# An attention kernel with a convolutional MoE layer behind it: the MoE begins at attention step 31, not 26, with its first-layer units 0.8 steps apart

## The chip, the core and the metric

One core of one Trainium2 chip runs the whole program. The time is device microseconds of one execution, from launch to end; the median of three runs is compared. A profile of one further execution is read beside it. Its five engines each work through a queue in order: PE (matmul; PEld is its weight load), DVE (vector), ACT (activations, copies out of PSUM), POOL (elementwise work in SBUF) and SP (issues DMAs).

## What is computed

Attention with rotary positions over 4 batches, 8 heads, 576 tokens, head width 64; its output, regrouped to 4 x 576 x 512, goes through a feed-forward layer with a gate that comes from a convolution over three neighbouring tokens:

```python
    q_rot, k_rot = (rotate(q), rotate(k))
    scores = scale * np.matmul(q_rot, k_rot.transpose(0, 1, 3, 2))
    scores = scores - np.max(scores, axis=-1, keepdims=True)
    attn = np.exp(scores)
    attn = attn / (np.sum(attn, axis=-1, keepdims=True) + 1e-09)
    return np.matmul(attn, v).astype(np.float32)
...
    h = np.maximum(x @ w_in, 0.0)
...
    for k in range(K):
        conv_out += conv_w[k][None, None, :] * hp[:, k:k + S, :]
    gate = 1.0 / (1.0 + np.exp(-conv_out))
    return (h * gate @ w_out).astype(np.float32)
```

All inputs are float32 but the three weight tensors of the layer, which arrive as 64-bit floats and are converted on the chip.

## The kernel before

**Attention steps.** The heads are taken two at a time: 16 pairs, numbered p, four to a batch. A pair takes five steps, s = 0 to 4, so that attention is steps n = 5p + s, 0 to 79. Step n holds the scores of 128 query rows (64 rows of both heads for s = 4) against all 576 keys (`emit_S`, L206 and L229, tile sp), a negated maximum on DVE (`reds`, L214, tile negm), the exponential with its sum on ACT (`exps`, L218, tile st), and the transposes of the exponentials of the step before (`emit_T`, L263, tile tp; ACT copies them out into pt at L162). In five steps there are also the transposes of the next pair's q, remainder and k (`emit_TQ`, L185 and L175), remainders (`emit_Trem`, L275 and L280, copied out by DVE), two products with v (`emit_E`, L316, for p in steps 5p+4 and 5p+5), the reciprocal of the sums and its way through HBM (`emit_rinv`, `emit_rinvT`, tiles sums, rvc, rst, rb), and in step 5p+8 the normalisation of both halves of the result (`norms`, L328, tile xn on DVE), which ACT and POOL split into the two parts of xT (L332, L333). POOL turns the next pair's q, r and k (`rope`, L143 to L156) eight and six steps ahead. Steps whose PE work has a product with v are called E steps below; they are two of every five.

**Slots of x.** xT has 12 slots of 128 columns of x by one half (290 tokens) of a batch. A normalisation takes a slot from `free_slots`, and the last first-layer unit of a block gives its four back (L349 to L351).

**The MoE.** A block is half of a batch, 288 tokens; there are eight. A block has eight first-layer units, M1 (`emit_M1`, f = 0 to 7): twelve matmuls with 290 columns (L347), Relu on ACT into one of four rr tiles (L355), and then, a number of ticks later by `lag`, the convolution on DVE (L359 once, L361 twice), tanh on ACT (L367), the gate on DVE (L370), and the split into g on ACT and POOL (L378, L379). Its second layer comes in units M2 (`emit_M2`) of six matmuls with 512 columns (L425), four units to a tile of 128 tokens; the tile stays in one of the two PSUM buffers of the pool m from its first unit to its fourth, when DVE copies it out (L432, tile ot).

**The order.** The whole program is written out in the order of a table: `at(n, rank, fn)` puts work into step n, and within a step the ranks sort it. Every engine works its queue in that order, with no later rearrangement. Until step WIDE the scores use a PSUM layout with 512 columns to a matmul and are emitted one step ahead; PSUM then has no pool m. During those steps the weights are converted in 16 pieces (`conv_w_piece`): an Abs on ACT (L443), four operations on DVE (L446, L452, L455, L460), and a copy on ACT and a subtraction on POOL (L503, L504). These units are spread evenly over steps 0 to WIDE-2 (`wsteps`). From WIDE on the scores take 288 columns to a matmul, the PSUM pool m is there, and MoE block number blk (of the first six) has its M1 units at n0+1+f and the M2 units of the block before from n0, with n0 = WIDE + 10 blk. Units of one step are spread between its transposes and products. The last two blocks come behind all of this (`seq`, `second`), all first-layer units and then all second-layer units.

**The convolution's weights.** `conv_cw` converts them (one Abs on ACT, four small operations on DVE, 32 x 128), and `turn_cw` turns them on PE (L524) and copies them out on DVE (L525).

The lines that the change touches are in this table's code:

```python
            for i, u in enumerate(wsteps):
                x = (WIDE - 1) * i // nw
                at(x, 0.4, u)
            at(12, 3, conv_cw)
            at(14, 2, turn_cw)
...
                us = [(n0 + 1 + f, lambda blk=blk, f=f: emit_M1(blk, f)) for f in range(NF)]
```

Of the kernel before, what the change touches and what calls it, by code (L numbers as in the profile page):

```python
# [20 lines left out]
def attention_moe_kernel(ctx, tc, q, k, v, w_in, conv_w, w_out, tab, out):  # L21
# [7 lines left out]
    NF = DFF // 128  # L29
# [138 lines left out]
    def emit_TQ(p, part):  # L168
# [5 lines left out]
        if part == "r":  # L174
# [3 lines left out]
            evac("A", KT[p][:, 0:64], ps[:, 64:128])  # L178
            if p * STEPS < WIDE:
                for h in range(2):  # L180
# [334 lines left out]
    def conv_cw():  # L515
        t = stage.pop("cw")
        w = late["ws"].tile([32, 128], F32, tag="cwf", name="cwf", bufs=1)
        for fn in to_f32(late["ws"], t, w, 128):
            fn()
        stage["cwf"] = w  # L520
# [12 lines left out]
    wcv = [conv_w_piece(i) for i in range(len(WPIECES))]  # L533
    wsteps = [wcv[0][0]]
    for i in range(len(wcv)):
        wsteps += [wcv[i + 1][0]] if i + 1 < len(wcv) else []
        wsteps += wcv[i][1:]

    WIDE = 26
    MB = 10  # L540
    plan = {}
    onpe = (0, 0.5, 1, 2, 4)
# [2 lines left out]
    def at(n, rank, fn):  # L545
        plan.setdefault(n, []).append((rank, len(plan.get(n, [])), fn))

    def emit():
        with tc.manual_schedule(engines=engines):
# [25 lines left out]
            for p in range(NP):  # L575
                n = STEPS * p
                for s in range(STEPS):
                    m = n + s
                    first = m < WIDE
                    if m:  # L580
# [3 lines left out]
                    for h in range(2 if s < 4 else 1):  # L584
                        at(m + 1, 0 if m + 1 < WIDE else 1, lambda p=p, s=s, h=h: emit_T(p, s, h))
                for g, e in ((0, 2), (1, 4), (2, 5)):
# [8 lines left out]
            for i, u in enumerate(wsteps):  # L595
                x = (WIDE - 1) * i // nw
                at(x, 0.4, u)
            at(12, 3, conv_cw)
            at(14, 2, turn_cw)
            moe = {}  # L600
            for blk in range(2 * B - 2):
                n0 = WIDE + MB * blk
                us = [(n0 + 1 + f, lambda blk=blk, f=f: emit_M1(blk, f)) for f in range(NF)]
                if blk:
                    m2 = m2_units(blk - 1)
                    ne = 8 if blk % 4 == 0 else 4
                    us += [(n0 + (i / ne if i < ne else 1.5 + 8.0 * (i - ne) / (len(m2) - ne)), u) for i, u in enumerate(m2)]
                for x, u in us:
                    moe.setdefault(int(x), []).append((x, u))
# [53 lines left out]
            for u in seq + second + m2_units(last) + m2_units(LASTB):  # L663
                u()
                tick()

    emit()


# [41 lines left out]
```

## Time and profile before

| | |
|---|---|
| median of three runs | 554.08 us (552.94 to 556.78) |
| the profiled execution | 554.89 us, of which the span of instructions is 553.1 us |
| PE busy | 508.9 us, 92% |
| DVE busy | 386.5 us, 70% |
| ACT busy | 325.1 us, 59% |
| POOL busy | 273.2 us, 49% |

Busy time of PE is modelled at its ends, so the pace of PE is better read from the distance between the starts of two instructions. The program has four stretches. From the start to 138.0 us there is attention alone (with the conversion of the weights); the scores of step 26, the first in the narrow layout, start there. Then come a first block of ten steps without second-layer units (to 193.2 us), four blocks with both layers (to 441.5 us, the scores of step 76), and the end of attention with the sixth block (to 490.3 us, where the first unit of the last two blocks starts).

### The profile page before, as it was taken

To read this page: it belongs to the slowest core of one execution; us is meant where nothing else is said; L and a number is where in the kernel's file an instruction comes from. 1 tells how busy PE (TensorE), PEld (TensorE's weight loads), DVE (VectorE), ACT (ScalarE), POOL (GpSimd) and SP (SyncE) were. 2 spreads that over 40 slices of the span, in tenths; PEclk is the share of its full clock that TensorE was granted. 3 is DMA by queue.
4 is the path that set the end of the run, shared out by engine and by line. 5 is a ranking of instruction groups with operands and counts; after the bars stand their busy time and mean duration, and the time that the engine had idled before them with its cause. 6 is when DMAs were issued, how large, how long until landed. Compare 5 with 4: busy or idle time off the path is not lost.

```text
span 553.1 us, 9298 instructions
## 1 busy us (share of the span) xinstructions
PE 508.9 (92%) x3295; PEld 369.3 (67%) x3295; DVE 386.5 (70%) x624; ACT 325.1 (59%) x870; POOL 273.2 (49%) x341
## 2 busy tenths in 40 slices
PE   2797969788999899999999999999999999999997
PEld 1354444445767477776877677777768677879986
DVE  4878977896588837684768747692677646657961
ACT  2779766877758545675747546663557546324530
POOL 4666857587573817383555637291361203232440
PEclk9999989999999999999999999999999999999999
DMA  7434433423303031030302140210300110000011
GB/s 187 130 101 130 121 104 97 142 75 71 87 1 87 1 83 24 24 84 7 99 2 66 40 106 1 62 45 26 101 0 24 41 42 0 29 33 20 2 38 58
DMA packets 67538, 33.08 MB, mean 60 GB/s; under 512 B 60412, under 2 KB 61220, under 8 KB 67492
## 3 DMA queue, kind: packets, MB, share of 16 engines
q1 hardware_dynamic: 66292, 32.10, 21.0%
q8 instruction: 26, 0.43, 0.3%
q10 hardware_dynamic: 1200, 0.39, 0.3%
q14 instruction: 20, 0.16, 0.1%
HBM read 27.68 MB, written 4.79 MB: 59 GB/s over the span
## 4 chain that ended last, share of the span: by engine, by line
PE 65%; DVE 15%; ACT 14%; issue 3%; DMA 2%; SPq 0%; ACTq 0%; DVEq 0%
PE tp L316 12%; PE sp L206 11%; PE pm L425 10%; PE pm L347 9%; PE tp L263 9%; PE mt L425 6%; ACT st L218 6%; PE mt L347 5%; DVE c L361 5%; ACT pt L162 4%; DVE negm L214 3%; DVE c L359 2%; PE tp L185 1%; DVE xn L328 1%; ACT wt L443 1%
## 5 line engine op out<-in xcount | busy, mean ns | idle before, releaser
L162 ACT ACTIVATE pt<-tp 128x512 f32<-128x512 f32 (+2 forms) x164 | 88.0, 562 | 93.1 <-PE tp L263 91.5
L214 DVE TENSOR_REDUCE negm<-sp 128x1 f32<-128x576 f32 x144 | 102.4, 748 | 39.5 <-PE sp L206 39.2
L379 POOL TENSOR_TENSOR g<-c,g 128x288 fp32r<-128x288 f32 (+4 forms) x88 | 57.0, 659 | 142.9 <-ACT g L378 141.3
L206 PE MATMUL sp<-kT,qT 64*128 64x288 f32 (+4 forms) x556 | 103.9, 470 | 1.2 <-ACT st L218 0.9
L218 ACT ACTIVATE st<-sp,negm 128x576 f32<-128x576 f32 x128 | 93.8, 746 | 15.1 <-DVE negm L214 15.1
L361 DVE SCALAR_TENSOR_TENSOR c<-rr,cw,c 128x288 f32<-128x288 f32 x128 | 96.7, 755 | 4.5
L263 PE MATMUL tp<-tabs,st 128*128 128x128 f32 x512 | 73.9, 285 | 20.3 <-ACT kr L162 7.6
L263 PEld LDWEIGHTS tp<-tabs,st 128*128 128x128 f32 x512 | 56.0, 143 | 46.2 <-issue 14.5
L347 PE MATMUL pm<-xT,winh 128*128 128x290 f32 x384 | 82.8, 308 | 0.5 <-ACT rr L355 0.5
L316 PE MATMUL tp<-pt,vm 128*64 128x290 f32 x512 | 69.6, 414 | 3.7 <-ACT pt L162 3.4
L206 PEld LDWEIGHTS sp<-kT,qT 64*128 64x128 f32 (+1 forms) x556 | 46.6, 177 | 36.0 <-issue 16.7
L425 PE MATMUL pm<-wouth,g 128*128 128x512 f32 x176 | 63.1, 412 | 0.0
L347 PEld LDWEIGHTS pm<-xT,winh 128*128 128x128 f32 x384 | 61.2, 190 | 1.4 <-ACT rr L355 0.7
L347 PE MATMUL pm<-xT,winl 128*128 128x290 f32 x192 | 56.9, 296 | 0.0
L370 DVE SCALAR_TENSOR_TENSOR c<-c,rr 128x288 f32<-128x288 f32 x64 | 39.1, 610 | 20.9 <-ACT c L367 20.2
L316 PEld LDWEIGHTS tp<-pt,vm 128*64 128x64 f32 x512 | 34.0, 136 | 28.8 <-ACT pt L162 5.1
L143 POOL TENSOR_TENSOR t<-rq,tabs 128x512 f32<-128x512 f32 x15 | 20.0, 1334 | 62.7 <-DMA rq<-q 62.1
L367 ACT ACTIVATE c<-c 128x288 f32<-128x288 f32 x64 | 28.3, 443 | 20.8 <-DVE c L361 20.5
L359 DVE TENSOR_SCALAR c<-rr,cw 128x288 f32<-128x288 f32 x64 | 31.2, 488 | 12.0 <-ACT rr L355 11.3
L425 PEld LDWEIGHTS pm<-wouth,g 128*128 128x128 f32 x176 | 33.1, 188 | 9.3 <-issue 2.2
L324 ACT ACTIVATE xn<-tp 128x290 f32<-128x290 f32 x32 | 13.2, 414 | 42.5 <-PE tp L316 42.5
L333 POOL TENSOR_TENSOR xT<-xn,xT 128x290 fp32r<-128x290 f32 x32 | 28.4, 892 | 18.2 <-ACT xT L332 16.9
(97 smaller groups left out, 883.6 us busy)
## 6 DMA issues: line engine op xcount, KB each, us to landing
out<-ot SPq DMA_DIRECT2D x17, 256.0 KB, 2.4
rk<-k SPq DMA_DIRECT2D x32, 128.0 KB, 3.0
w<-moe_w_in SPq DMA_DIRECT2D x8, 512.0 KB
vm<-v SPq DMA_DIRECT2D x32, 128.0 KB, 2.4
w<-moe_w_out SPq DMA_DIRECT2D x8, 512.0 KB, 3.4
rq<-q SPq DMA_DIRECT2D x30, 128.0 KB, 2.5
rb<-rd SPq DMA_DIRECT2D x16, 144.0 KB, 2.9
rb<-rd SPq DMA_DIRECT2D x16, 128.0 KB, 3.0
```

The lines of the kernel that those rows point to most:

```text
L162: nc.scalar.activation(out=out, in_=in_, func=AF.Copy, scale=1.0 if sc is None else sc)
L206: nc.tensor.matmul(out=out, lhsT=qt[64 * h:64 * h + 64, c], rhs=kt[64 * h:64 * h + 64, a:a + n], start=True, stop=True)
L214: reds.setdefault((p, s), []).append(lambda: nc.vector.tensor_reduce(out=nm, in_=sc, axis=AX.XY if len(sc.shape) == 3 else AX.X, op=ALU.ma ...
L218: lambda: nc.scalar.activation(out=dst, in_=sc, func=AF.Exp, bias=nm, scale=1.0, accum_out=sm)
L263: nc.tensor.transpose(ps[:, 128 * t:128 * t + 128], st[:, 128 * t:128 * t + 128], idf)
L316: nc.tensor.matmul(out=xp[64 * h:64 * h + 64, 0:XW], lhsT=vmain[p][:, h, i, :] if i < 4 else vrem[p % 2][:, h, :], rhs=PT[p][:, 2 * i + h ...
L347: nc.tensor.matmul(out=ps[:, 0:XW], lhsT=w[:, kk, fs], rhs=xT[:, xs, e, :], start=(i == 0), stop=(i == n - 1))
L359: nc.vector.tensor_scalar(out=c, in0=r[:, j:j + HS], scalar1=cw[:, f:f + 1], scalar2=None, op0=ALU.mult)
L361: nc.vector.scalar_tensor_tensor(out=c, in0=r[:, j + e:j + e + HS], scalar=cw[:, 8 * e + f:8 * e + f + 1], in1=c, op0=ALU.mult, op1=ALU.add,)
L370: nc.vector.scalar_tensor_tensor(out=c, in0=c, scalar=1.0, in1=r[:, j + 1:j + 1 + HS], op0=ALU.add, op1=ALU.mult)
L379: nc.gpsimd.tensor_tensor(out=lo, in0=c[:, o:o + n], in1=hi.bitcast(F32), op=ALU.subtract)
L425: nc.tensor.matmul(out=ops[tt][:, 0:width], lhsT=g_tile(tt, f, e), rhs=w[:, f, cols], start=(f == 0 and i == 0), stop=(f == NF - 1 and i = ...
```

## The change

Three things are changed. WIDE goes from 26 to 31, so that the wide layout lasts five steps longer, the conversion of the weights is spread over 30 steps instead of 25, and every MoE block begins five steps later. The M1 units of a block stand 0.8 steps apart instead of 1. And `conv_cw` moves from the end of step 12 into the list of conversion units, behind the eighth piece (which puts it into step 15), with `turn_cw` in step 18 instead of 14.

```diff
-        wsteps += wcv[i][1:]
-
-    WIDE = 26
+        wsteps += wcv[i][1:] + ([lambda: conv_cw()] if i == 7 else [])
+
+    WIDE = 31
...
-            at(12, 3, conv_cw)
-            at(14, 2, turn_cw)
+            at(18, 2, turn_cw)
...
-                us = [(n0 + 1 + f, lambda blk=blk, f=f: emit_M1(blk, f)) for f in range(NF)]
+                us = [(n0 + 1 + 0.8 * f, lambda blk=blk, f=f: emit_M1(blk, f)) for f in range(NF)]
```

Two places show how this moves instructions. The first is DVE's queue around the conversion of the convolution's weights (tile wt of 32 x 128 and cwf). Before, between the maxima of steps 12 and 13:

```order
L214 TENSOR_REDUCE negm<-sp 128x1 x2
L460 SCALAR_TENSOR_TENSOR wf<-w_515,wt 128x512
L446 TENSOR_SCALAR wt<-wt 32x128
L452 TENSOR_SCALAR wt<-wt 32x128
L455 SCALAR_TENSOR_TENSOR wt<-cw_177,wt 32x128
L460 SCALAR_TENSOR_TENSOR cwf<-cw_177,wt 32x128
L214 TENSOR_REDUCE negm<-sp 128x1 x2
```

Now, between the maxima of steps 15 and 16:

```order
L214 TENSOR_REDUCE negm<-sp 128x1 x2
L446 TENSOR_SCALAR wt<-wt 32x128
L452 TENSOR_SCALAR wt<-wt 32x128
L455 SCALAR_TENSOR_TENSOR wt<-cw_177,wt 32x128
L460 SCALAR_TENSOR_TENSOR cwf<-cw_177,wt 32x128
L289 TENSOR_SCALAR sums<-sums 128x9
L290 RECIPROCAL rvc_82<-sums 128x9
L214 TENSOR_REDUCE negm<-sp 128x1 x2
```

The four small operations now stand alone between two maxima, without a piece of the other weights, and in an E step.

The second is DVE's queue late in the second block (tiles c, rr and cw belong to the convolution, L370 is the gate, the copy at L164 takes a remainder out of PSUM). Before, between the maxima of steps 42 and 43:

```order
L214 TENSOR_REDUCE negm<-sp 128x1 x2
L370 SCALAR_TENSOR_TENSOR c<-c,rr_1421 128x288
L164 COPY pt<-tp 128x256
L359 TENSOR_SCALAR c<-rr_1422,cw 128x288
L361 SCALAR_TENSOR_TENSOR c<-rr_1422,cw,c 128x288 x2
L214 TENSOR_REDUCE negm<-sp 128x1 x2
```

Now, at the same place of the five-step cycle, between the maxima of steps 47 and 48:

```order
L214 TENSOR_REDUCE negm<-sp 128x1 x2
L359 TENSOR_SCALAR c<-rr_1630,cw 128x288
L361 SCALAR_TENSOR_TENSOR c<-rr_1630,cw,c 128x288 x2
L370 SCALAR_TENSOR_TENSOR c<-c,rr_1629 128x288
L164 COPY pt<-tp 128x256
L359 TENSOR_SCALAR c<-rr_1631,cw 128x288
L361 SCALAR_TENSOR_TENSOR c<-rr_1631,cw,c 128x288 x2
L370 SCALAR_TENSOR_TENSOR c<-c,rr_1630 128x288
L214 TENSOR_REDUCE negm<-sp 128x1 x2
```

Two units' convolutions and gates stand there where one unit's stood. On PE the units of a block that stood one to a step in eight steps stand now in six steps of ten (two of the six hold two); the last three steps hold none but one second-layer unit. Attention's last step is unchanged, so that behind it there are now the eight first-layer units of the sixth block and twelve second-layer units, where part of them stood among the steps 76 to 79 before.

## Rows read from the trace of the kernel before

**Rows 1.** The page: busy time of each engine over the whole span.

```profile
PE 508.9 (92%) x3295; PEld 369.3 (67%) x3295; DVE 386.5 (70%) x624; ACT 325.1 (59%) x870; POOL 273.2 (49%) x341
```

**Rows 2.** Busy time by stretch: the stretch, its length, busy us of PE, PEld, DVE, ACT, POOL (instructions), the granted TensorE clock, DMA share, GB/s.

```profile
32.80:129.40 96.60, 79.19 (x499) 44.58 (x498) 84.80 (x111) 75.02 (x197) 64.89 (x66) 0.96 0.39 111
70.00:84.00 14.00, 8.66 (x44) 4.91 (x42) 9.60 (x14) 10.07 (x29) 7.21 (x7) 0.79 0.36 102
138.00:193.20 55.20, 51.30 (x362) 36.84 (x360) 42.72 (x67) 36.34 (x95) 34.68 (x47) 1.00 0.18 44
193.20:441.50 248.30, 245.51 (x1659) 182.92 (x1657) 166.77 (x282) 148.10 (x400) 116.66 (x148) 1.00 0.18 47
441.50:490.28 48.78, 46.20 (x287) 36.07 (x285) 27.93 (x53) 22.71 (x63) 13.49 (x21) 1.00 0.07 24
```

**Rows 3.** PE's timeline at the scores that open the two E steps of each five, attention alone: start, us, line, operation, tiles.

```profile
32.75 0.39 PE L229 MATMUL sp<-kr,qT 128*128 128x128 f32 x2
...
55.14 0.39 PE L229 MATMUL sp<-kr,qT 128*128 128x128 f32 x2
...
81.96 0.63 PE L229 MATMUL sp<-kr,qT 128*128 128x128 f32 x2
...
106.50 0.39 PE L229 MATMUL sp<-kr,qT 128*128 128x128 f32 x2
...
129.40 0.39 PE L229 MATMUL sp<-kr,qT 128*128 128x128 f32 x2
```

**Rows 4.** The chain of work that ended last, attention alone: a product with v in an E step, and ACT's work in a step that is none: start, us, what.

```profile
39.39 2.59 PE tp L316 x20
...
122.46 1.45 ACT st L218 x4
123.91 0.55 ACT wt L443
```

**Rows 5.** The timeline around the conversion of the convolution's weights, DVE and PE; in brackets the idle time before and what ended it.

```profile
73.98 1.19 DVE L446 TENSOR_SCALAR wt<-wt 32x128 f32<-32x128 f32 x1 [3.48 <-ACT wt L443]
...
76.97 1.40 DVE L214 TENSOR_REDUCE negm<-sp 128x1 f32<-128x576 f32 x2
...
79.29 1.11 PE L263 MATMUL tp<-tabs,st 128*128 128x128 f32 x4 [3.62 <-ACT st L218]
```

**Rows 6.** PE's timeline in two steps of the second block: scores, transposes, the first matmuls of M1 units and the transpose behind one, and, last, scores that took longer.

```profile
203.56 0.52 PE L347 MATMUL pm<-xT,winh 128*128 128x290 f32 x2
...
205.26 0.27 PE L175 MATMUL tp<-tabs,t 128*128 128x128 f32 x1
...
207.09 1.24 PE L206 MATMUL sp<-kT,qT 64*128 64x288 f32 x8
208.26 1.09 PE L263 MATMUL tp<-tabs,st 128*128 128x128 f32 x8
209.10 0.52 PE L347 MATMUL pm<-xT,winh 128*128 128x290 f32 x2
...
211.54 1.19 PE L206 MATMUL sp<-kT,qT 64*64 64x288 f32 x8
...
235.77 1.87 PE L206 MATMUL sp<-kT,qT 64*128 64x288 f32 x8
```

**Rows 7.** The chain of work that ended last, at the first second-layer units.

```profile
195.47 1.39 PE pm L425 x6
196.86 0.44 PE tp L185 x4
```

**Rows 8.** DVE's groups of instructions in the stretch 201.5 to 262.0 us: shapes, count, busy us, mean ns of one, idle before.

```profile
L361 DVE SCALAR_TENSOR_TENSOR c<-rr,cw,c 128x288 f32<-128x288 f32 x16 | 13.4, 836 | 0.6
L370 DVE SCALAR_TENSOR_TENSOR c<-c,rr 128x288 f32<-128x288 f32 x8 | 5.0, 630 | 2.0 <-ACT c L367 1.8
L359 DVE TENSOR_SCALAR c<-rr,cw 128x288 f32<-128x288 f32 x8 | 3.6, 454 | 2.0 <-ACT rr L355 1.8
L164 DVE COPY pt<-tp 128x256 f32<-128x256 f32 (+1 forms) x8 | 2.5, 314 | 3.6 <-PE tp L275 2.9 <-PE tp L280 0.7
```

**Rows 9.** DVE's timeline at two convolutions of the second block.

```profile
206.34 0.37 DVE L359 TENSOR_SCALAR c<-rr,cw 128x288 f32<-128x288 f32 x1
206.75 3.05 DVE L361 SCALAR_TENSOR_TENSOR c<-rr,cw,c 128x288 f32<-128x288 f32 x2
209.72 1.41 DVE L214 TENSOR_REDUCE negm<-sp 128x1 f32<-128x576 f32 x2
...
223.88 0.46 DVE L370 SCALAR_TENSOR_TENSOR c<-c,rr 128x288 f32<-128x288 f32 x1
...
224.75 1.07 DVE L361 SCALAR_TENSOR_TENSOR c<-rr,cw,c 128x288 f32<-128x288 f32 x2
```

**Rows 10.** POOL's timeline beside them.

```profile
206.76 1.28 POOL L143 TENSOR_TENSOR t<-rq,tabs 128x512 f32<-128x512 f32 x1 [9.34 <-DMA rq<-q]
208.11 1.37 POOL L149 TENSOR_TENSOR rq<-rq,tabs 128x512 f32<-128x512 f32 x1
...
226.84 0.94 POOL L379 TENSOR_TENSOR g<-c,g 128x224 fp32r<-128x224 f32 x2 [3.56 <-ACT g L378]
```

**Rows 11.** PE's timeline behind attention: two waits.

```profile
478.11 0.54 PE L347 MATMUL pm<-xT,winh 128*128 128x290 f32 x2 [0.50 <-ACT rr L355]
...
489.48 0.50 PE L425 MATMUL mt<-wouth,g 128*128 128x512 f32 x1 [1.16 <-ACT g L378]
```

## The prediction, made before the changed kernel ran

> **What bounds the kernel now.** The page is read first: PE is busy 92% of the span, no other engine over 70% [rows 1]. That share is an average over stretches, so the busy times by stretch come next [rows 2]. From 193.20 to 441.50 us, four blocks with both layers, PE works 245.5 of 248.3 us: its work sets the pace there. In attention alone, 32.80 to 129.40 us, it works 79.2 of 96.6 us, DVE 84.8 and ACT 75.0: none is full, and the chain goes round ACT, PE and DVE. In the first block, 138.00 to 193.20 us, PE works 51.3 of 55.2 us. So a step of attention is cheaper beside the MoE, as long as PE stays full there. The change moves five attention steps to where PE idles, and gives the weights' conversion more steps. Its sum is the price of five more steps alone, less what they no longer cost beside the MoE, plus the waits that closer M1 units make.
>
> **1. Five more steps alone: +15.5 us.** Five steps, from the scores that open one pair's E steps to those of the next, take 22.39 us (32.75 to 55.14), 26.82, 24.54 and 22.90 us (106.50 to 129.40) [rows 3]. The middle two hold the conversion of the convolution's weights. There DVE waits 3.48 us for ACT's Abs, its small operations last from 73.98 to 76.97 us, the maxima behind them come late, and PE waits 3.62 us for the exponentials [rows 5]; the granted clock in 70 to 84 us is 0.79, a stretch partly at the lower of its levels, 1.2 GHz [rows 2]. An undisturbed round is the mean of the other two, 22.65 us.
>
> In steps that are no E step the chain runs over two exponentials, 1.45 us, and the Abs of a weight piece, 0.55 us [rows 4]. By ACT's order before, fifteen such operations (an Abs, or the copy of a piece, taken at the same 0.55) stand in the twelve such steps of the four rounds: 2.0 us a round. Spread over 30 steps instead of 25 they are 5/6 of it: 0.34 us less, 22.3 us a round. `conv_cw` now stands in step 15 with only the sums behind it. Its wait is shorter, since the Abs stands right behind the exponentials on ACT, and the E step covers it: between the scores of step 16 and the transposes that need its exponentials PE has a product of 2.59 us [rows 4]. I take nothing for it; without the cover it would again be up to the 4.2 us by which the second round exceeds 22.65. `turn_cw` has its copy on DVE behind four operations of a piece and one normalisation of step 18, while the transposes behind it need that PSUM buffer: 0 to 3 us, taken as 1.0.
>
> Before, four rounds, 32.75 to 129.40, take 96.65 us; now five take 111.5 + 1.0, and the first steps are 0.3 us shorter. Step 31 starts as late behind its last round as step 26 did, so it starts 15.5 us later (bounds 12 with rounds of 21.8 us and nothing for `turn_cw`, 19.6 with 22.65 and 3 us).
>
> **2. First block: -1.0 us.** It takes 55.2 us; a later block takes (248.3 - 4 x 1.39) / 4 = 60.7 us (the last of the four has four M2 units more than the eight of the others, at 1.39 [rows 7]), and 49.6 without its M2 units. So 5.6 us are lost in the first block, where DVE and POOL are busy 42.7 and 34.7 us [rows 2]. Closer M1 units add a wait of about 3.4 us at its end (by the working of part 3, with 1.4 us less PE work), but its last three steps hold no unit, so that DVE catches up. If it does, 49.6 + 3.4 = 53.0 us; if not, 55.2 or 1 us more. I take 54.2.
>
> **3. Four blocks: +4.4 us.** PE's work in a block is the same. What changes is DVE's queue between the maxima of n0+6 and n0+7 (47 and 48 in the second block): two convolutions and two gates for one of each. Count from the scores of step 47. They last 1.17 us (207.09 to 208.26), transposes 0.84, an M1 unit 1.70 (203.56 to 205.26), an M2 unit 1.39 [rows 6, 7]; with 0.44 us for the smaller transposes of each step, step 48 starts at 4.15 and step 49 could at 8.0 us. DVE makes the maxima of 47 from 1.2 to 2.6 us, then a convolution (0.45 + 2 x 0.84 = 2.13), a gate (0.63), the copy (0.31), a convolution and a gate [rows 8]: at 8.4 us the maxima of 48 begin. Half of them and one exponential, 0.7 us each [rows 4, 9], free the PSUM buffer at 9.9: step 49 waits 1.9 us. With the shortest rows (convolution 0.37 + 1.07, gate 0.46) it is 0.2 us; with both convolutions like the one at 206.34 us (0.37 + 3.05) it is 4.5 [rows 9]. I take 2.0. Behind the late maxima stand a normalisation, the copy of an output tile and a gate; the E step that follows covers them. Before, too, a block pays here: the step at 207.09 takes 4.45 us for 4.15 of work, and the scores at 235.77 take 1.87 instead of 1.24 us [rows 6], 0.9 together. So each block gets 1.1 us longer (bounds -0.7 and +3.6).
>
> The Trainium skill, page "SBUF — State Buffer", section "Who interferes with whom", says that a DVE instruction with two SBUF inputs and a GpSimd instruction that reads SBUF shut each other out, the later one waiting for the whole of the earlier. The trace agrees: the pair of 206.75 us took 3.05 us beside POOL's rotation of q (206.76 and 208.11), the pair of 224.75 us 1.07 us with POOL idle before 226.84 [rows 9, 10]. That rotation is issued at the end of step 47, so by this rule the second convolution would be the long one in each block. Its price is that of the first rival.
>
> **4. The end: -16.9 us.** Step 80, the tenth of the fifth block, has no scores, and there is no seventeenth pair to transpose: 1.17 + 2 x 0.44, 2.0 us less. From the scores of step 76 to the last two blocks it was 48.8 us [rows 2], with four steps of attention in it. Now eight M1 and twelve M2 units remain, 8 x 1.70 + 12 x 1.39 = 30.3 us. Four M1 units stand directly behind another while an M2 tile holds the second PSUM buffer: 0.5 us each, as at 478.11 [rows 11]. The last M2 units wait for g, since eight convolutions with their gates, 2.76 us each [rows 8], outlast PE: 1.16 us at 489.48 [rows 11], now 0 to 4, taken as 1.6. Together 33.9 us, 14.9 less.
>
> **Sum.** 15.5 - 1.0 + 4.4 - 2.0 - 14.9 = +2.0 us. On the profiled execution, 554.89 us with a span of 553.1, that is 556.9; it lies 0.8 us above the median of 554.08, which gives 556.1 us.
>
> The slots of x cost nothing: with 0.8 steps the eighth unit of a block stands in n0+6, one step ahead of the normalisation that takes its slots. Queue time on SP is no term either: the same DMAs are issued, and weight pieces wait longer for buffers that nobody is waiting for.
>
> **The rivals.** *DVE becomes the bound where the units are close.* For it: six steps hold eight units at 2.76 us of DVE each, and the first block already loses 5.6 us. Against it: over four whole blocks DVE works 166.8 of 248.3 us. If the second convolution alone is long, the wait is 2.4 to 3.2 us: part 3 is up to 9.2, 561 us. If both are, 4.5 us: part 3 is 14.4, 566 us. It decides from a wait of 2.9 us on, where the sum passes +5.5.
>
> *Attention alone runs freely.* The conversion is what holds ACT and DVE there. If all 2.0 us of it leave the chain, a round is 20.7 us, part 1 is +7.5; with waits of 0.9 us, which cost a block what it pays already, part 3 is 0. The sum is then -10.4, 544 us; with rounds of 21.5 us it is -6.4, 548 us. For it: the chain spends only about a tenth on conversion, and thinner conversion may let it slip. Against it: E steps are full of PE work and three others full of ACT work either way. It decides below 21.7 us a round with no new wait in part 3.
>
> *Nothing is gained or lost.* Waits move from the first block and the end into the middle: 554 us. It lies within the forecast.
>
> **How the numbers follow.** Differences within 1% (5.5 us) can hardly be told from none here. The likeliest is the sum, 556.1 us, within 1%: 0.50. The first rival, slower by more: 0.29. The second, faster by more: 0.21. Eight times in ten it should lie between 547 and 564 us: the ends leave out both convolutions long and rounds of 20.7 us.
>
> **What would show it.** Scores of step 31 at 153.5 us; rounds of 22.3 us with no 3.5 us wait of DVE before a 32 x 128 operation; the first block 54 us, four blocks 250.7 us, the end 34 us behind them. Wrong would be PE idle for over 3 us before the scores of steps 49, 59, 69 and 79, or rounds under 21.7 us.

## The result, and the profile of the changed kernel

The changed kernel takes 562.23 us (median of four runs, 558.95 to 565.40) where the kernel before takes 553.81 (four runs beside them, 552.94 to 556.78). The ratio is 1.0125, with a 95% interval from 1.0083 to 1.0167: slower by about 6.9 us (the two medians alone are 8.4 us apart). The forecast was 556.1 us. Its range, 547 to 564 us, holds the result; the ratio lies above its likeliest case, a difference within 1%, though the interval reaches into it.

The profiled execution took 565.40 us, the longest of the four, with a span of 563.5 us, 10.4 more than the span of before. The four executions differ with their mean granted clock: 565.40 us at 0.985, 563.04 at 0.991, 561.43 at 0.993 and 558.95 at 0.997. So the profile below shows more of the lower clock than the median does. The page first: busy times, the answer to [rows 1].

```profile
PE 513.3 (91%) x3287; PEld 371.9 (66%) x3287; DVE 355.2 (63%) x619; ACT 326.7 (58%) x877; POOL 269.3 (48%) x341
```

PE's work has grown by 4.4 us in 10.4, and DVE is busy 31.3 us less. But for five more steps in the wide layout the instructions are the same in another order; the time is in waits, and in stretches at a lower clock.

Busy time by stretch, the answer to [rows 2] (stretch, length, busy us of PE, PEld, DVE, ACT and POOL, granted clock, DMA share, GB/s): five rounds of attention alone, two pieces of 14 us in them, the first block, the next three blocks, and the rest up to the first unit of the last two blocks.

```profile
32.73:149.30 116.57, 98.62 (x623) 56.38 (x622) 85.13 (x126) 91.28 (x241) 74.28 (x80) 0.97 0.37 102
84.00:98.00 14.00, 10.62 (x60) 6.13 (x58) 8.99 (x16) 8.88 (x24) 6.16 (x9) 0.88 0.13 34
98.00:112.00 14.00, 12.63 (x74) 7.24 (x76) 12.12 (x19) 11.29 (x31) 11.53 (x13) 0.88 0.44 135
157.85:213.90 56.05, 51.76 (x364) 37.45 (x362) 39.23 (x68) 36.69 (x96) 34.58 (x48) 0.97 0.18 43
213.90:399.90 186.00, 179.60 (x1226) 134.30 (x1224) 116.23 (x210) 111.29 (x304) 95.59 (x124) 1.00 0.19 48
399.90:500.71 100.81, 96.37 (x586) 75.03 (x585) 52.78 (x106) 44.92 (x122) 20.78 (x31) 0.98 0.08 26
```

In the three blocks PE idles 6.4 of 186.0 us; over the four blocks of [rows 2] it idled 2.8 of 248.3. The granted clock is 1.00 in the three blocks, 0.97 in the first block and 0.98 in the rest; before it was 1.00 in all of them.

PE's timeline at the scores that open the rounds, and at those of step 31 (last line), the answer to [rows 3]:

```profile
32.74 0.39 PE L229 MATMUL sp<-kr,qT 128*128 128x128 f32 x2
...
55.28 0.39 PE L229 MATMUL sp<-kr,qT 128*128 128x128 f32 x2
...
77.74 0.39 PE L229 MATMUL sp<-kr,qT 128*128 128x128 f32 x2
...
104.88 0.39 PE L229 MATMUL sp<-kr,qT 128*128 128x128 f32 x2
...
127.50 0.39 PE L229 MATMUL sp<-kr,qT 128*128 128x128 f32 x2
...
149.33 0.39 PE L229 MATMUL sp<-kr,qT 128*128 128x128 f32 x2
...
157.93 0.51 PE L206 MATMUL sp<-kT,qT 64*128 64x288 f32 x2
```

The rounds take 22.54, 22.46, 27.14, 22.62 and 21.83 us. Four of them have a mean of 22.4, as forecast (22.3). The third holds the conversion of the convolution's weights and is 4.8 us longer. Its timeline, the answer to [rows 5], on DVE, ACT and PE:

```profile
85.02 0.30 ACT L443 ACTIVATE wt<-cw 32x128 f32<-32x128 f32 x1
85.35 0.23 DVE L446 TENSOR_SCALAR wt<-wt 32x128 f32<-32x128 f32 x1 [2.61 <-ACT wt L443]
...
86.36 1.24 DVE L460 SCALAR_TENSOR_TENSOR cwf<-cw,wt 32x128 int32<-32x128 int32 x1
...
87.62 0.67 ACT L443 ACTIVATE wt<-w 128x512 f32<-128x512 f32 x1 [2.31 <-DVE cwf L460]
...
88.19 0.43 ACT L162 ACTIVATE pt<-tp 64x64 f32<-64x64 f32 x2
...
88.67 1.09 PE L316 MATMUL tp<-pt,vr 128*64 128x290 f32 x4 [2.19 <-ACT pt L162]
...
89.70 1.97 PE L263 MATMUL tp<-tabs,st 128*128 128x128 f32 x8
```

DVE's wait of 2.61 us is there, as forecast. What was not forecast stands on ACT. Its next instruction is the Abs of a weight piece, which writes a tile `wt`; `wt` has two buffers, one held by the piece in work, the other by the conversion. So the Abs waits 2.31 us until DVE's last operation of the conversion has read it, and behind it in ACT's queue stands the copy of transposed exponentials that PE's product needs. PE waits 2.19 us in the middle of the E step, the granted clock of 84 to 98 us and of 98 to 112 us is 0.88, partly at 1.2 instead of 2.4 GHz, and the transposes at 89.70 us take 1.97 us, where the same eight take 1.09 us at 208.26 us in [rows 6].

Where the units are closer, PE's waits before scores, in total us, number, longest (PE's waits over the whole span; in the kernel before they are 0.9 us in 3, the longest 0.4):

```profile
PE sp L206 <- ACT st L218: 6.5, 6, 2.2
```

The largest, at step 39 in the first block; DVE, POOL and PE:

```profile
198.06 1.50 POOL L143 TENSOR_TENSOR t<-rq,tabs 128x512 f32<-128x512 f32 x1
198.35 1.52 DVE L370 SCALAR_TENSOR_TENSOR c<-c,rr 128x288 f32<-128x288 f32 x1
...
199.79 1.41 DVE L214 TENSOR_REDUCE negm<-sp 128x1 f32<-128x576 f32 x2
...
201.46 2.18 PE L206 MATMUL sp<-kT,qT 64*64 64x288 f32 x8 [2.25 <-ACT st L218]
```

Behind this wait the granted clock falls (the stretch from 196 to 210 us):

```profile
196.00:210.00 14.00, 10.96 (x66) 6.48 (x65) 8.67 (x11) 8.25 (x23) 11.28 (x14) 0.88 0.17 39
```

And at steps 48 and 49 in the second, where the forecast looked for it:

```profile
259.47 1.54 PE L206 MATMUL sp<-kT,qT 64*128 64x288 f32 x8
...
260.54 1.36 DVE L361 SCALAR_TENSOR_TENSOR c<-rr,cw,c 128x288 f32<-128x288 f32 x2
...
262.04 1.51 POOL L143 TENSOR_TENSOR t<-rq,tabs 128x512 f32<-128x512 f32 x1
262.32 1.41 DVE L214 TENSOR_REDUCE negm<-sp 128x1 f32<-128x576 f32 x2
263.63 1.60 POOL L149 TENSOR_TENSOR rq<-rq,tabs 128x512 f32<-128x512 f32 x1
264.25 1.19 PE L206 MATMUL sp<-kT,qT 64*64 64x288 f32 x8 [0.38 <-ACT st L218]
264.62 0.93 DVE L370 SCALAR_TENSOR_TENSOR c<-c,rr 128x288 f32<-128x288 f32 x1
```

The same place in the third and in the fifth block, steps 59 and 79:

```profile
326.55 1.19 PE L206 MATMUL sp<-kT,qT 64*64 64x288 f32 x8 [1.22 <-ACT st L218]
...
456.90 1.64 PE L206 MATMUL sp<-kT,qT 64*64 64x288 f32 x8 [1.91 <-ACT st L218]
```

The second convolution's pair takes 1.36 us, not 3 as at 206.75 us in [rows 9]: POOL's rotation begins when it is over. In place of the pair, a gate stands beside the rotation: 1.52 us at 198.35 and 0.93 at 264.62 us. The Trainium skill, page "SBUF — State Buffer", section "Who interferes with whom", has the later of two such instructions wait for the whole of the earlier. The trace agrees in the main: the two gates end 0.31 and 0.32 us after POOL's operation (a gate without POOL's work beside it takes 0.45 us). Only the victim is another than the forecast took.

PE's waits behind attention, the answer to [rows 11]:

```profile
478.75 0.53 PE L347 MATMUL pm<-xT,winh 128*128 128x290 f32 x2 [0.50 <-ACT rr L355]
...
481.13 0.53 PE L347 MATMUL pm<-xT,winh 128*128 128x290 f32 x2 [0.50 <-ACT rr L355]
...
486.59 0.53 PE L347 MATMUL pm<-xT,winh 128*128 128x290 f32 x2 [0.56 <-ACT rr L355]
...
491.99 0.53 PE L347 MATMUL pm<-xT,winh 128*128 128x290 f32 x2 [0.50 <-ACT rr L355]
500.71 0.42 PE L347 MATMUL mt<-xT,winh 128*128 128x290 f32 x2
```

Four waits of half a microsecond, as forecast, and none for g. From 500.71 us to the end of the span it is 62.8 us, as from 490.28 us before.

### The profile page after: what moved, and what is told of

Same layout as the page of the kernel before. It is cut to its first block, busy times and chain, and to the rows that moved or that the text cites. A ratio compares the mean times of both kernels' runs of the same rounds, so it can differ in the third digit from the quotient of the medians.

```text
span 563.5 us, 9284 instructions
## 1 busy us (share of the span) xinstructions
PE 513.3 (91%) x3287; PEld 371.9 (66%) x3287; DVE 355.2 (63%) x619; ACT 326.7 (58%) x877; POOL 269.3 (48%) x341
## 4 chain that ended last, share of the span: by engine, by line
PE 74%; ACT 13%; DVE 8%; issue 2%; DMA 1%; SPq 0%; ACTq 0%; DVEq 0%
PE tp L316 15%; PE sp L206 13%; PE pm L347 12%; PE pm L425 10%; PE tp L263 9%; PE mt L425 7%; ACT st L218 5%; PE mt L347 5%; ACT pt L162 4%; DVE negm L214 2%; PE tp L185 1%; DVE c L370 1%; DVE c L361 1%; ACT wt L443 1%; DMA rq<-q 1%
## 5 line engine op out<-in xcount | busy, mean ns | idle before, releaser
L162 ACT ACTIVATE pt<-tp 128x512 f32<-128x512 f32 (+2 forms) x168 | 89.4, 556 | 76.9 <-PE tp L263 75.9
L263 PE MATMUL tp<-tabs,st 128*128 128x128 f32 x512 | 76.0, 291 | 19.3 <-ACT kr L162 8.7
L263 PEld LDWEIGHTS tp<-tabs,st 128*128 128x128 f32 x512 | 57.9, 146 | 45.8 <-issue 13.8
L361 DVE SCALAR_TENSOR_TENSOR c<-rr,cw,c 128x288 f32<-128x288 f32 x128 | 81.5, 637 | 4.5
L206 PEld LDWEIGHTS sp<-kT,qT 64*128 64x128 f32 (+1 forms) x540 | 45.1, 178 | 37.8 <-issue 19.4
L370 DVE SCALAR_TENSOR_TENSOR c<-c,rr 128x288 f32<-128x288 f32 x64 | 39.6, 622 | 14.7 <-ACT c L367 14.6
L355 ACT ACTIVATE rr<-pm 128x289 f32<-128x289 f32 x48 | 20.1, 419 | 33.5 <-PE pm L347 33.5
L359 DVE TENSOR_SCALAR c<-rr,cw 128x288 f32<-128x288 f32 x64 | 26.9, 421 | 17.7 <-ACT rr L355 17.6
L347 PEld LDWEIGHTS pm<-xT,winl 128*128 128x128 f32 x192 | 36.6, 191 | 0.0
```

The lines of the kernel that those rows point to most:

```text
L162: nc.scalar.activation(out=out, in_=in_, func=AF.Copy, scale=1.0 if sc is None else sc)
L206: nc.tensor.matmul(out=out, lhsT=qt[64 * h:64 * h + 64, c], rhs=kt[64 * h:64 * h + 64, a:a + n], start=True, stop=True)
L263: nc.tensor.transpose(ps[:, 128 * t:128 * t + 128], st[:, 128 * t:128 * t + 128], idf)
L347: nc.tensor.matmul(out=ps[:, 0:XW], lhsT=w[:, kk, fs], rhs=xT[:, xs, e, :], start=(i == 0), stop=(i == n - 1))
L359: nc.vector.tensor_scalar(out=c, in0=r[:, j:j + HS], scalar1=cw[:, f:f + 1], scalar2=None, op0=ALU.mult)
L361: nc.vector.scalar_tensor_tensor(out=c, in0=r[:, j + e:j + e + HS], scalar=cw[:, 8 * e + f:8 * e + f + 1], in1=c, op0=ALU.mult, op1=ALU.add,)
```

## The experiments

Every run has the kernel before beside it on the same chip. On the chips of the experiments that takes 555.3 to 556.5 us, so kernels are compared by their ratios to it. Four numbers of each profile tell where the time is: the start of the first scores in the narrow layout (step WIDE), the length of the first block, of the three blocks behind it, and of all the rest to the end of the span.

| kernel | ratio to before (95%) | narrow scores start | first block | three blocks | rest |
|---|---|---|---|---|---|
| before | 1 | 138.0 | 55.2 | 182.1 | 177.8 |
| changed | 1.0125 (1.0083 to 1.0167) | 157.9 | 56.0 | 186.0 | 163.6 |
| e1_cw_own | 1.0094 (1.0061 to 1.0127) | 153.9 | 55.4 | 186.5 | 162.3 |
| e2_cw_split | 1.0053 (1.0025 to 1.0080) | 153.5 | 55.7 | 186.0 | 163.5 |
| e3_no_cw | 1.0048 (1.0024 to 1.0072) | 152.6 | 55.4 | 186.1 | 162.4 |
| e8_a_split_095 | 1.0045 (1.0021 to 1.0070) | 153.6 | 53.5 | 187.7 | 161.7 |
| e4_units_08 | 1.0032 (1.0005 to 1.0058) | 138.3 | 54.5 | 185.6 | 176.9 |
| e5_b_split | 0.9853 (0.9818 to 0.9888) | 131.2 | 54.0 | 182.4 | 177.8 |
| e12_b_split_08 | 0.9938 (0.9914 to 0.9963) | 131.9 | 54.5 | 186.3 | 177.0 |
| e9_b_norm9 | 1.0239 (1.0199 to 1.0279) | 147.3 | 57.6 | 184.6 | 176.7 |
| e10_norm9_31 | 1.0372 (1.0345 to 1.0399) | 171.6 | 57.9 | 184.4 | 159.4 |
| e6_b_split_29 | 1.0045 (1.0018 to 1.0072) | 144.1 | 53.8 | 186.2 | 173.7 |
| e7_b_split_24 | 1.0047 (1.0025 to 1.0070) | 125.0 | 53.6 | 186.2 | 190.2 |
| e11_b_split_21 | 1.0144 (1.0116 to 1.0171) | 121.7 | 55.6 | 187.3 | 197.5 |

A difference of 1 us between two profiles can be the granted clock alone: `e1_cw_own`, `e2_cw_split` and `e3_no_cw` have the same program from step 31 on, and their rests differ by 1.2 us. The theory after the result had three parts: the conversion's stall stayed (theory 1), closer units cost (theory 2), and the move itself loses (theory 3).

### What the conversion costs in step 15: three runs

The first, `e1_cw_own`, gives `conv_cw` a tile of its own:

```diff
-    def to_f32(pool, w64, w, n):
+    def to_f32(pool, w64, w, n, tag="wt"):
...
-        t = pool.tile([128, n], I32, tag="wt", name="wt")[0:w64.shape[0]]
+        t = pool.tile([128, n], I32, tag=tag, name=tag, bufs=2 if tag == "wt" else 1)[0:w64.shape[0]]
...
-        for fn in to_f32(late["ws"], t, w, 128):
+        for fn in to_f32(late["ws"], t, w, 128, "wtc"):
```

> The changed kernel, with a temporary tile of its own for the convolution's weights, so that the Abs of the next weight piece has no buffer to wait for. Theory 1 (the buffer): that Abs is what holds ACT's queue, and the copies and exponentials behind it; the third round goes from 27.2 to about 23.5 us and the time from 562.2 to about 558.5 us. Rival 1 (the wait of DVE): what costs is that DVE waits for the conversion's own Abs with the maxima queued behind it; the round stays at 26 to 27 us, the time at 561 to 562 us.

The timeline of this run around the conversion:

```profile
84.50 0.30 ACT L443 ACTIVATE wtc<-cw 32x128 f32<-32x128 f32 x1
84.71 0.68 ACT L443 ACTIVATE wt<-w 128x512 f32<-128x512 f32 x1
84.84 0.23 DVE L446 TENSOR_SCALAR wtc<-wtc 32x128 f32<-32x128 f32 x1 [2.91 <-ACT wtc L443]
...
85.30 0.43 ACT L162 ACTIVATE pt<-tp 64x64 f32<-64x64 f32 x2
...
85.80 0.68 PE L316 MATMUL tp<-pt,vr 128*64 128x290 f32 x4
```

The Abs of the weight piece follows at once, the copy comes 0.8 us behind the conversion's Abs instead of 3.2, and PE does not wait. DVE still waits, 2.91 us, and it matters little (the next run takes that wait away and the round gets 0.7 us shorter). The third round, 77.22 to 100.90 us, takes 23.7 us, by theory 1. The ratio moved less than expected (0.3%, and the two intervals overlap), so it is the trace that decides here, not the time.

The second, `e2_cw_split`, also puts DVE's part later, behind the end of the next weight piece; in the trace that is between the maxima of steps 17 and 18, two steps later and not one:

```diff
-        for fn in to_f32(late["ws"], t, w, 128):
-            fn()
-        stage["cwf"] = w
+        fns = to_f32(late["ws"], t, w, 128, "wtc")
+        fns[0]()
+        stage["cwf"], stage["cwr"] = w, fns[1:]
+
+    def end_cw(piece):
+        piece()
+        for fn in stage.pop("cwr"):
+            fn()
...
         wsteps += wcv[i][1:] + ([lambda: conv_cw()] if i == 7 else [])
+        if i == 8:
+            wsteps[-1] = lambda fn=wsteps[-1]: end_cw(fn)
```

> The changed kernel, the conversion with a tile of its own and cut in two: its Abs stays in step 15, DVE's four small operations stand one step later, behind the end of a weight piece, so DVE has nothing to wait for. Theory 1 (the buffer): third round about 23 us, hardly less than with the tile alone. Rival 1 (the wait of DVE): only here it falls, from 26 to 27 us with the tile alone to about 23 us. Both give about 558 us. Rival 2 (the round is long whatever the conversion does, by the clock or the E step): 27 us, 562 us.

The third round is 23.0 us, 0.7 less than with the tile alone (part of which may be the granted clock, 0.93 over that round in `e1_cw_own` and 1.00 here), and step 31 starts at 153.5 us, the forecast's number. The ratio falls to 1.0053, 0.7% or 4.0 us below the changed kernel.

The third, `e3_no_cw`, leaves the convolution's weights out:

```diff
-        wsteps += wcv[i][1:] + ([lambda: conv_cw()] if i == 7 else [])
+        wsteps += wcv[i][1:]
...
-            load_cw()
+            nc.gpsimd.memset(cw, 0.25)
...
-            at(18, 2, turn_cw)
```

> The changed kernel without the convolution weights' load, conversion and transposition (the weights are set to one constant, so this part of the computation is left out): the bound of what any arrangement of them can give back. Theory 1 and rival 1: every round 22.0 to 22.7 us, step 31 starts at 152.5 to 153.5 us, the time is 556.5 to 558 us. Rival 2: a round of 26 us or more remains, 561 us or more.

Its third round takes 22.0 us and its ratio is 1.0048, no different from the conversion in two pieces. The 1.0 us that the round still gets shorter lies in step 19: in `e2_cw_split` PE waits there 1.49 us for DVE's copy of the turned weights (`turn_cw`), here 0.53 us for a copy of ACT. So next to the stall the conversion costs too little to show in the time, and half a per cent of loss against the kernel before remains that it has nothing to do with.

### What closer units cost, and what the conversion cost before

`e4_units_08` takes the kernel before and changes the spacing alone:

```diff
-                us = [(n0 + 1 + f, lambda blk=blk, f=f: emit_M1(blk, f)) for f in range(NF)]
+                us = [(n0 + 1 + 0.8 * f, lambda blk=blk, f=f: emit_M1(blk, f)) for f in range(NF)]
```

> The kernel before with first-layer units 0.8 steps apart and nothing else. Theory 2 (close units cost): each of the five blocks beside attention is about 1.3 us longer, as after the change, with new waits of PE before the scores of the eighth and ninth step of a block; 559 to 561 us. Rival (the blocks got longer for another reason, such as how far the other work has come by then): 553 to 555 us, the same as before.

The three blocks are 3.5 us longer, 1.2 each, as after the change, though the rest of the kernel is as before. The first block and the rest give back 1.6 us, so that the ratio is 1.0032: in time this is nearer to the rival, while the trace shows the longer blocks and the waits of theory 2.

`e5_b_split` takes the kernel before with the conversion in two pieces; MoE from step 26, units 1 step apart:

```diff
         wsteps += wcv[i][1:]
+        if i == 7:
+            wsteps[-1] = lambda fn=wsteps[-1]: (fn(), conv_cw())
+        if i == 8:
+            wsteps[-1] = lambda fn=wsteps[-1]: end_cw(fn)
...
-            at(12, 3, conv_cw)
-            at(14, 2, turn_cw)
+            at(18, 2, turn_cw)
```

with `conv_cw`, `end_cw` and `to_f32` as in `e2_cw_split`.

> The kernel before (MoE from step 26, units 1 step apart) with the conversion of the convolution's weights in two pieces and a tile of its own, as in the second experiment. Theory 1 (the conversion's stall is in the kernel before as well, some 6 us in its second and third round): scores of step 26 at 132 to 133 us instead of 138, the time 1.0% below before. Then the five steps alone cost about 21 us at the start, not 15.5, and the move itself loses. Rival (the stall only moves to the rounds behind it or into the first block): step 26 at 135 us or later, or the first block at 58 us; within 0.4% of before.

It is the fastest kernel of the study: 547.47 us, 1.5% below before, more than theory 1 said. Step 26 starts at 131.2 us, 6.8 earlier (0.9 of it ahead of step 5, where the two programs are the same), the first block is 1.2 us shorter, for which no run gives the reason, and all behind it is as before. So the kernel before paid a stall at its conversion too. It took another way there: DVE waited 3.48 us for the Abs, and the maxima behind it came late [rows 5]. Which of the differences takes it away (the tile of its own, DVE's part two steps later, `turn_cw` four steps later) no run separates.

`e12_b_split_08` is this kernel with the spacing of 0.8 (the diff of `e4_units_08`):

> The fifth experiment's kernel (MoE from step 26, conversion in two pieces) with units 0.8 steps apart; against the second experiment it has only the start five steps earlier. If the spacing costs what the fourth experiment showed (0.3%), it takes 549 to 550 us, and the move alone, from here to the second experiment, costs 1.6 to 1.7%, 9 us. Rival (the spacing is the larger part, 1 us a block and more in the first and at the end): 552 to 554 us, and the move costs 1.0%, 5.5 us.

It comes nearer to the rival: 0.9938 against 0.9853 is 0.9%, 4.7 us, of which 3.9 lie in the three blocks. Its waits of PE before scores:

```profile
PE sp L206 <- ACT st L218: 5.1, 7, 2.2
```

In `e5_b_split` they are 1.1 us in 3. In the three blocks PE idles 6.4 us in `e12_b_split_08` and 2.5 in `e5_b_split`, which is the whole difference: 1.5 us of it before scores, 1.7 before products that wait for DVE's copy of a remainder (L164), 0.75 before transposes. That DVE has too much to do is not the reason. Its two largest groups in the three blocks (count, busy us, mean ns, idle before them and for what), in the kernel before:

```profile
L361 DVE SCALAR_TENSOR_TENSOR c<-rr,cw,c 128x288 f32<-128x288 f32 x48 | 39.8, 829 | 1.7
L214 DVE TENSOR_REDUCE negm<-sp 128x1 f32<-128x576 f32 x54 | 38.5, 750 | 13.0 <-PE sp L206 12.8
```

and in the changed kernel:

```profile
L214 DVE TENSOR_REDUCE negm<-sp 128x1 f32<-128x576 f32 x54 | 38.6, 751 | 35.9 <-PE sp L206 35.9
L361 DVE SCALAR_TENSOR_TENSOR c<-rr,cw,c 128x288 f32<-128x288 f32 x48 | 32.9, 686 | 1.7
```

The convolutions are shorter, and DVE idles 35.9 instead of 12.8 us for scores. Its work comes in a burst behind two units and then stops: the burst makes the maxima and the copy of the remainder late, and the time saved elsewhere is of no use.

`e8_a_split_095` tries another spacing on `e2_cw_split`, with one step of a block holding two units instead of two such steps:

```diff
-                us = [(n0 + 1 + 0.8 * f, lambda blk=blk, f=f: emit_M1(blk, f)) for f in range(NF)]
+                us = [(n0 + 0.3 + 0.95 * f, lambda blk=blk, f=f: emit_M1(blk, f)) for f in range(NF)]
```

> The second experiment's kernel (MoE from step 31, conversion in two pieces) with first-layer units from n0 + 0.3 on, 0.95 steps apart, so that only one step of a block holds two of them instead of two. Theory 2 (two units in one step make DVE's maxima late): blocks of 60.5 to 61 us instead of 62, 4 to 5 us below the second experiment, 0.8% less. Rival (the wait moves to the step with the two units): blocks of 62 us, within 0.3% of the second experiment.

The rival held: the waits before scores fall from 6.5 to 2.3 us, but M1 units wait 5.2 us for a PSUM buffer (2.1 in `e2_cw_split`), the three blocks take 187.7 us, and the time is the same.

### What the move itself costs

The pair `e12_b_split_08` and `e2_cw_split` differs in the start of the MoE, and in how the conversion is spread, which hangs on it. The later start is slower by 1.0053 / 0.9938 = 1.0116, 6.4 us. In the two profiles the narrow scores start 21.6 us later, the first block is 1.2 us longer, and the rest is 13.5 us shorter. That makes 9.0 us, of which 2.3 are the lower clock: the granted clock is 0.88 behind the waits of steps 39 and 79 in the profile of `e2_cw_split`, and 1.00 from step 26 to the end in that of `e12_b_split_08`.

A second pair has units 1 step apart. From step 31 on this needs slots of x that are not there, so both kernels of the pair normalise one step later. `e9_b_norm9` is `e5_b_split` with

```diff
-                    at(n + 8, 1.7 + j, lambda p=p, j=j: norms.pop((p, j))())
+                    at(n + 9, 2.5 + 0.2 * j, lambda p=p, j=j: norms.pop((p, j))())
```

> The fifth experiment's kernel (MoE from step 26, units 1 step apart, conversion in two pieces) with each pair's normalisation one step later, in n + 9 behind the first transposes. It is the ground for the next run, which needs this to have slots. Expected within 0.4% of the fifth experiment, 545 to 550 us; over 552 us would mean that ACT waits for the slot in its place in the order.

This was wrong by far, 1.0239. PE's largest wait in it is a new one:

```profile
PE tp L263 <- ACT xn L324: 9.9, 2, 5.3
```

The reason stands on ACT, whose copy of the product waits for one of the three buffers of `xn` until POOL has read what was normalised in it:

```profile
ACT xn L324 <- POOL xT L333: 16.8, 3, 6.3
```

It is the stall of the changed kernel's conversion in another place: an instruction that waits for a buffer, at the head of an engine's queue.

`e10_norm9_31` is that kernel with `WIDE = 31`:

> The ninth experiment's kernel with the MoE from step 31 and nothing else: units stay 1 step apart, and the place of the units against the E steps is the same. Theory 3 (the move itself loses): step 31 starts 22 us later than step 26 does in the ninth, blocks of 60.5 to 61 us, first block 54, and the end gives back some 16 us; 6 us above the ninth, 1.1%. Rival (only the closer units lose): the end gives back 20 us or more; within 0.4% of the ninth.

The ratio of the two is 1.0130, 7.2 us. The narrow scores start 24.3 us later, the first block differs by 0.3 us, the three blocks by 0.1, and the rest is 17.3 us shorter. So with units 1 step apart the move leaves the blocks as they are: their lengthening is the spacing's alone. In both pairs the later start loses, as theory 3 has it. The second price is the less clean one: the waits for `xn` make single rounds 28.2 and 31.9 us long in `e9_b_norm9` and 29.4 in `e10_norm9_31`, whose last is 28.9 us, and the 24.3 us hold the difference.

### Three other starts, which tell less

`e6_b_split_29` and `e7_b_split_24` are `e5_b_split` with `WIDE = 29` and `WIDE = 24`.

> The fifth experiment's kernel with the MoE from step 29 instead of 26, units still 1 step apart. Theory 3 (a step alone, 4.5 us, is dearer than what it adds beside the MoE, (60.7 less 10 units of 1.70 and 1.39 in their numbers, 24.7) / 10 = 3.6 us): 3 x 0.9 = 2.7 us above the fifth experiment, 0.5% more. Rival (the end gives back what the start costs): the same as the fifth within 0.2%.

> The fifth experiment's kernel with the MoE from step 24, the weights' conversion in 23 steps. Theory 3: 2 x 0.9 = 1.8 us below the fifth experiment, 0.3% less. Rival (the end gives it back, or the closer conversion and the first block lose it): the same or above.

They give 1.0045 and 1.0047, nearly 11 us above `e5_b_split` on either side. In the first neither expectation came true, in the second the rival's; neither run tests the price of a step. Steps of attention repeat every five, and a start that is not five steps off sets the units against other steps: the three blocks take 186.2 us in both instead of 182.4, and PE waits 7.5 and 5.3 us before scores. In the second, the denser conversion also puts operations of a weight piece in front of maxima that stand ahead of them in `e5_b_split`. DVE's timeline there:

```profile
19.02 1.28 DVE L446 TENSOR_SCALAR wt<-wt 128x512 f32<-128x512 f32 x1 [2.26 <-ACT wt L443]
20.33 0.83 DVE L452 TENSOR_SCALAR wt<-wt 128x512 int32<-128x512 int32 x1
21.20 1.10 DVE L455 SCALAR_TENSOR_TENSOR wt<-w,wt 128x512 int32<-128x512 int32 x1
22.22 1.41 DVE L214 TENSOR_REDUCE negm<-sp 128x1 f32<-128x576 f32 x2
```

The maxima come behind them, PE waits 3.0 us, and the fourth scores start at 27.2 instead of 22.9 us.

`e11_b_split_21` starts five steps earlier than `e5_b_split`, in the same place against attention's steps:

```diff
-    WIDE = 26
+    WIDE = 21
...
-                us = [(n0 + 1 + f, lambda blk=blk, f=f: emit_M1(blk, f)) for f in range(NF)]
+                us = [(n0 + 3 + 0.75 * f, lambda blk=blk, f=f: emit_M1(blk, f)) for f in range(NF)]
```

> The fifth experiment's kernel with the MoE from step 21, the weights' conversion in 20 steps; units of the first layer 0.75 steps apart from n0 + 3 on, since the normalised rows come no earlier. Theory 3: one round less at the start, some 22 us, against 16 at the end, and about 1 us a block for the closer units: 545 to 547 us. Rival (what the move gives, the denser conversion and the first block lose): 550 us or more.

The rival held, 1.0144: the narrow scores start at 121.7 us, only 9.5 earlier, since with the conversion in 20 steps the scores of step 5 come 5.1 us later and the rounds are 23.8, 24.6 and 27.0 us long. An earlier start is no gain as long as the weights have to be converted in it.

## Why the prediction was right or wrong

By its own terms, in the two profiled executions:

| term | forecast | measured |
|---|---|---|
| 1. step 31 starts later than step 26 did | +15.5 | +19.9 |
| 2. first block | -1.0 | +0.8 |
| 3. three of the four blocks | +3.3 | +4.0 |
| 3 and 4. fourth block and the end (1.1 - 2.0 - 14.9) | -15.8 | -14.2 |
| sum | +2.0 | +10.4 |

The 10.4 us are those of the longest of four executions. Of them 2.6 are the lower clock behind two waits (1.4 in the first block, 1.2 behind step 79, worked out below); the ratio, 6.9 us, is the better measure of the whole.

**The step that failed is `conv_cw` in part 1.** The prediction said of DVE's wait for the Abs that "the E step covers it" and that "I take nothing for it". About DVE's wait that was right within 0.7 us: in `e1_cw_own` it lasts 2.91 us and the round is 23.7, and 23.0 without it. But it followed only the engine on which a wait had been seen before. It did not follow the tile: with `wt` in two buffers the next instruction on ACT had to wait for the conversion as well, and ACT's queue feeds the product inside that same E step. The third round is 4.8 us over the mean of the others, of which 3.5 go with the tile of its own (27.1 to 23.7) and 0.7 with DVE's part two steps later. The sentence beside it, that without the cover it would be up to 4.2 us, had the size nearly right, and the 1.0 us taken for `turn_cw` is what the round gets shorter without it (23.0 us in `e2_cw_split`, 22.0 in `e3_no_cw`). With the conversion mended, step 31 starts at 153.5 us, the forecast's time to the tenth, with rounds of 22.5, 22.5, 23.0, 22.6 and 21.8 us.

The sum also hid the loss of the move, which the two pairs show. It set the end, -16.9, against +15.5 at the start, and this +15.5 was one more round less, in the main, a stall of 6.1 us (96.65 - 4 x 22.65) that the change was expected to remove. The price of the move alone, five steps at 22.3 us in all against 16.9 at the end, is 5.4 us in the prediction's own numbers, and 6.4 and 7.2 in the two pairs. So the change could only be neutral if the stall went, and `e5_b_split` shows that the stall goes without the move.

**Part 2 is off by 1.8 us, of which 1.4 are the clock.** The wait of about 3.4 us that it expected came as 2.25 us at step 39, with a gate beside POOL's rotation ahead of the maxima. `e4_units_08` and `e12_b_split_08` have the same spacing and a wait of 2.24 us at that place, but a granted clock of 1.00 behind it (here of `e12_b_split_08`):

```profile
174.00:186.00 12.00, 9.48 (x70) 5.56 (x72) 7.25 (x13) 7.84 (x20) 11.43 (x15) 1.00 0.01 2
```

There the block takes 54.5 us, where the forecast said 54.2. Step by step the changed kernel's first block is that of `e12_b_split_08` within 0.02 us, but for the step of the wait: 7.32 us with the clock at 0.88, 5.88 with 1.00. The prediction had no term for the clock behind a wait. Whether closer units lengthen the first block stays open: it is 0.7 us shorter in `e4_units_08` than in the kernel before, and 0.5 us longer in `e12_b_split_08` than in `e5_b_split`.

**Part 3 was right**, in size and as a cost of the spacing: +1.1 us a block forecast, 1.3 measured, 1.2 in `e4_units_08` and 1.3 in `e12_b_split_08`, and nothing from the move (`e10_norm9_31`). The place was only half right. The scores of steps 49, 59, 69 and 79, where it looked for 2.0 us, wait 0.38, 1.22, 0.38 and 1.91 us. The E step that was to cover what stands behind the late maxima waits as well: over the three blocks 0.75 us before transposes and 2.26 before products that need DVE's copy of a remainder (0.56 in the kernel before).

**Part 4** named four waits of 0.5 us and they are there; the wait for g that it counted, 1.6 us, is not. Fourth block and end together give back 1.6 us less than forecast, and 1.2 of that is again the clock: behind the wait of step 79 it is 0.88 (448 to 462 us). `e1_cw_own` and `e3_no_cw`, with the same program from step 31 on and the same wait (1.92 us), have 1.00 there, and their rest takes 162.3 and 162.4 us instead of 163.6.

**The rivals.** The time lies near the first rival's 561 us, but its mechanism is not what happened: the convolutions got shorter, and part 3 is near its forecast value. So it is luck that the range holds the time: its upper end was set for a stall that did not come, and left room for one that nobody had counted. The second rival falls: even without the conversion of the convolution's weights the five rounds take 21.8 to 22.6 us (`e3_no_cw`), not 20.7 or 21.5.

By ratios, the whole change can be split into four parts: the old stall leaves (`e5_b_split`, 0.9853), the units come closer (`e12_b_split_08` to it, 1.0086), the MoE starts five steps later (`e2_cw_split` to that, 1.0116), and the conversion makes its new stall (the changed kernel to that, 1.0072): -8.1, +4.7, +6.4 and +4.0 us. That their product is the whole is no check, since the kernels between cancel. All but the first rest on two kernels that were not timed side by side, each only against the kernel before, and are good to some 0.4% or 0.5%. For the last the two intervals all but touch; the trace of the round, 27.1 and 23.0 us, supports it.

The rest of `e2_cw_split` is only 13.5 us shorter than that of `e12_b_split_08`, where the pair with units 1 step apart has 17.3. The traces give most of these 3.8 us: 1.2 are the clock behind step 79, and 1.7 the wait before its scores, 1.92 us in `e2_cw_split`, 0.18 in `e12_b_split_08` and none in `e10_norm9_31`. The last 0.9 us stay open.

## What to carry to other kernels

When an operation is moved, follow its buffers as well as its engine: ask which instruction takes the next buffer of each of its tiles, on which queue that one stands, and what is queued behind it. When a sum comes out near zero because a stall is to vanish, price the removal of the stall by itself, since it may be had without the rest; here the conversion in two pieces with a tile of its own gave 1.5% where the whole change lost 1.25%. And in a schedule with a period (five steps here), compare only starts that keep the units' place in it, and expect that doubling up units makes a neighbouring engine late even while its busy time falls. Before a term of the sum is blamed for a miss, read the granted clock of its stretch: the same wait of PE cost 1.4 us more in one profile than in another.

## What the runs showed of the hardware that was not expected

DVE's busy time fell by 31.3 us without any operation less in the MoE. Half of it, 15.2 us, lies in the convolution's multiply-adds (L361), 9.8 in the conversion of the weights. In the three blocks a multiply-add took 829 ns on the mean before and 686 after, the operation and its shape being the same. The reason is meetings with POOL's work. Counted by start and end, 42 of the 48 had an instruction of POOL beside them before (873 ns on the mean), 30 after (786); those without one took 519 ns in both kernels. And a wait of PE of 2.19 us inside attention alone was followed by a granted clock of 0.88 in two stretches of 14 us; with the tile of its own, which takes that wait away, the round is 3.5 us shorter, not 2.2, with 0.93 instead of 0.87 as the round's granted clock. Such a wait does not always bring the clock down: behind the 2.25 us at step 39 it was 0.88, behind the 2.24 us of `e12_b_split_08` 1.00.
